# Tests for saturated tanh values moved ahead of the gate products, and those products written over the tanh values, in a fused attention and convolution-gated feed-forward kernel

## The chip, the cores and the metric

The kernel runs on one core of a Trainium2 chip. The metric is the device time of one execution in microseconds (us). The engines of the core are TensorE (PE in the profile, with its weight loads as PEld), VectorE (DVE), ScalarE (ACT), GpSimd (POOL) and SyncE (SP). They run side by side, each in the order of its own instruction list, and wait for one another through semaphores.

## The reference

Attention for 4 batches, 8 heads, 768 positions and a head width of 64, with a local window of 96 keys, 8 global keys and a bias that grows with distance; its heads side by side are the 512 columns of x. Then a feed-forward block with a gate that comes from a convolution along the sequence (w_in is 512 x 1024, w_out 1024 x 512, hp is h padded by one row at each end):

```python
    scores = np.where(keep, scores, -1000000000.0)
    scores = scores - np.max(scores, axis=-1, keepdims=True)
    a = np.exp(scores)
    a = a / (np.sum(a, axis=-1, keepdims=True) + 1e-09)
    return np.matmul(a, v).astype(np.float32)
...
    x = np.ascontiguousarray(attn_out.transpose(0, 2, 1, 3)).reshape(B, S, H * D)
...
    h = np.maximum(x @ w_in, 0.0)
    ...
    for k in range(K):
        conv_out += conv_w[k][None, None, :] * hp[:, k:k + S, :]
    gate = 1.0 / (1.0 + np.exp(-conv_out))
    return (h * gate @ w_out).astype(np.float32)
```

## The kernel before, in words

**Attention** runs as a pipeline of 96 steps: 32 jobs (a batch, a half of the sequence, a pair of heads) of three blocks of 128 queries. A step s goes through `scores` (L395, PE, into one of two PSUM buffers "s"), `maxima` (L412, DVE), `exps` (L426, ACT, into one of three buffers `pbuf`), `normalise` (L437 and L438 on DVE, L444 on POOL, in early steps also L442 on ACT), two steps later `transposes` (L452, PE, into one of two PSUM buffers "t"), `evict` (L457, ACT), and per job `values` (L473, PE), `mixed_high` (L485, ACT) and `mixed_low` (L489, DVE).

**The feed-forward block** runs in 8 units n = 0 to 7, one for each half sequence of 384 tokens. `mm1` (L507, PE) makes the features in 8 blocks f, each from three products of high and low parts of fp32 numbers; `relu` (L517, ACT) puts half of them into `hbuf`. `conv` (L557 on POOL or, in the first two units, L555 on ACT; then L558 and L559 on DVE) adds the three taps in the tile `c`, of which there is one buffer. `gate` (L577, ACT) takes the tanh of `c` in place, in four groups of two blocks. `saturated` (L588, ACT) reads the tanh values of one group once more and counts, in a column of `low`, how near they are to where an approximation would not hold; its elementwise result goes to a tile nobody reads (`sat`, tag "ob", which is also the only buffer of the output tiles of L629). `split` works on 128 tokens t at a time: L610 (DVE) makes (c + 1) * h, L612 (ACT) rounds it to `gh`, L613 (DVE) puts the rest into `gl`. `mm2` (L622, PE) multiplies both with the output weights in 24 products per 128 tokens; L629 evicts, L630 sends. The last 128 tokens of all go through `last_tile` (L643) and `leave` (L652, L655).

Where L610 writes is decided in `split`: over `h` in `hbuf` in the odd units and in parts that end before the unit does, over `c` in the last part of an even unit. As `saturated` reads `c`, a product that writes `c` has to wait for it.

**The order of work.** `ffn` writes a list of the unit's calls. A convolution, gate or test follows the products of a later block; what is left when `mm1` is over (`post`) is dealt out among the 24-product tiles of `mm2` of the unit before, at the positions that `AT` gives: the first row for even units, the second for odd ones.

```python
        at = AT[n % 2]
        for k, a in enumerate(mm):
            items.append(a)
            ...
            while post and at[-len(post)] <= k + 1:
                items.append(post.pop(0))
```

Unit 0 has no `mm2` beside it; its `post` is kept in `late` and runs within `mm1` of unit 1. The attention steps draw calls from this list. The first 16 steps stand in an order that is written out by hand; after them a scheduler orders each engine's list from the order of the calls, what they depend on and what it reckons that they take. Weight checks (L346 on DVE, L350 on ACT) and a final flag (L363 to L366, L895, L896) stand beside this; the flag is not waited for by the products.

Of the kernel before, what the change touches and what calls it, by code (L numbers as in the profile page):

```python
# [32 lines left out]
HF, NG = NF // 2, 4  # L33
NU, SPU = 2 * B, NPAIR * NB
# [11 lines left out]
DECODE_BY_HAND, DECODE_LATER = (0.3, 1.2), (1.35,)  # L46
FIRST_LOADS = (0, 0, 1, 2)
SHARE = (0.3, 0.5)
AT = ((2, 4, 9, 16, 17, 25), (1, 2, 4, 5, 7, 12, 16))


def key_columns(u):
# [15 lines left out]
def fast_path(tc, io):  # L68
# [422 lines left out]
    def ends(s):  # L491
        return s >= 0 and s % NB == NB - 1
# [72 lines left out]
    WG = NF // NG  # L565
# [27 lines left out]
    def split(n, t):  # L593
        b = n // 2
        t0, t1 = bounds[n % 2]
        a0, a1 = max(t0, t * P), min(t1, (t + 1) * P)
        if (b, t) not in gt:
            gt[b, t] = (
                pg.tile([P, NF, P], F32R, tag="gh", name=f"gh{b}_{t}"),
                pg.tile([P, NF, P], F32R, tag="gl", name=f"gl{b}_{t}"),  # L600
            )
        gh, gl = gt[b, t]
        c = cbuf[n][:, :, a0 - t0 : a1 - t0]
        sl = slice(a0 - t * P, a1 - t * P)
        h = hbuf[:, :, a0 + 1 : a1 + 1]
        if exact:
            V.scalar_tensor_tensor(c, c, 2.0, h, ALU.mult, ALU.mult)
        else:
            x = h if n % 2 or a1 < t1 else c
            V.scalar_tensor_tensor(x, c, 1.0, h, ALU.add, ALU.mult)  # L610
            c = x
        cur["gated"] = A.activation(gh[:, :, sl], c, AF.Copy)  # L612
        V.tensor_tensor(gl[:, :, sl], c, gh[:, :, sl].bitcast(F32), ALU.subtract)  # L613
# [44 lines left out]
    def ffn(n, defer=True):  # L658
        items = []
        add = lambda cost, fn, *a: items.append((cost, fn, a))  # L660
        early, lag = late[:], 1 + len(late) // 2
        late.clear()
        for f in range(NF):
            for part in range(3):
                if n or f >= EARLY or not begun[0]:
                    add(1, mm1, n, f, part)
                elif part == 0:
                    for k in range(begun[0], NK):
                        add(1, mm1_slice, f, k)
                if part == 1:  # L670
                    if early:
                        items.append(early.pop(0))
                    if f >= lag:
                        add(0, conv, n, f - lag)
                if part == 2:
                    g = f - lag + 1
                    if g > 0 and g % WG == 0:
                        add(0, gate, n, g // WG - 1)
                    g -= 1
                    if g > 0 and g % WG == 0 and n < NU - 1:  # L680
                        add(0, saturated, n, [g // WG - 1])
        old = tiles_of(n - 1) if n else []
        post = [(0, conv, (n, f)) for f in range(NF - lag, NF)] + [(0, gates, (n,))]
        post += [(0, split, (n, t)) for t in parts_of(n)]
        post.insert(len(post) if n == NU - 1 else lag + 3, (0, saturated, (n, range(NG))))
        mm = [(1, mm2, (b, t, f)) for b, t in old for f in range(NF)]
        if not mm and defer:
            late.extend(post[lag:])
            return items + post[:lag]
        if not mm:  # L690
            return items + post
# [3 lines that stand above are left out]
            if k == 0:  # L695
                for x in range(lag - 1):
# [3 lines that stand above are left out]
        return items + post  # L700

    def tiles_of(n):
        b = n // 2
        return [(b, t) for t in ((0, 1) if n % 2 == 0 else (2, 3, 4, 5))]

    def parts_of(n):
        return (0, 1, 2) if n % 2 == 0 else (2, 3, 4, 5)
# [77 lines left out]
    for s in range(len(steps) + LAG_V + 1):  # L785
        cur["s"] = s
        m, i = steps[s] if s < len(steps) else (len(jobs), -1)
        if s < HAND:
# [5 lines left out]
            x = (s - LAG_V - 1) // NB if ends(s - LAG_V - 1) else None  # L794
# [27 lines left out]
        else:  # L822
# [10 lines left out]
            if e >= 0:  # L833
                if e % SPU == SPU - 1:
                    queue.extend(ffn(e // SPU))
                left = SPU - (e + 1) % SPU + 1
                if e + 1 >= len(steps) - SPU:
                    left += 1
                k = -(-sum(cost for cost, _, _ in queue) // left)
# [67 lines left out]
    def general():  # L907
# [27 lines left out]
        for n in range(NU):  # L935
# [31 lines left out]
            for _, fn, a in ffn(n, defer=False):  # L967
                fn(*a)
# [98 lines left out]
```

## Time and profile before

| | |
|---|---|
| median of three runs | 446.5 us (445.61, 446.50, 447.54) |
| profiled execution, its own time | 445.31 us |
| its span on the core | 443.5 us, mean granted TensorE clock 0.996 |
| PE busy | 431.2 us, 97% of the span |
| DVE busy | 357.2 us, 81% |
| ACT busy | 309.9 us, 70% |
| POOL busy | 221.2 us, 50% |
| last PE instruction ends | 440.1 us into the span |

The span is what the profiler saw of one execution; 1.8 us of the execution's own time lie around it. Busy time is the time in which an instruction of an engine is under way. PE's matmuls overlap one another, so one that is listed with 0.40 us may start 0.23 us after the one before it.

### The profile page before, as it was taken

How to read it: one execution, taken by the hardware profiler on the slowest of the kernel's cores; microseconds unless marked ns; L12 is line 12 of the kernel's file. 1: busy time of each engine (PE TensorE's matmuls, PEld its weight loads, DVE VectorE, ACT ScalarE, POOL GpSimd, SP SyncE). 2: the span in 40 equal slices, each digit the busy share in tenths (PEclk: the TensorE clock that was granted, in tenths of full speed). 3: DMA queues.
4: the chain of work that ended last, by engine and by line, in shares of the span. 5: the costliest groups of instructions: out<-in, count | busy, mean ns of one | idle time of the engine just before them, and what ended most of it. 6: DMA issues, size and time to landing. Idle time of an engine off the chain costs nothing.

```text
span 443.5 us, 9050 instructions
## 1 busy us (share of the span) xinstructions
PE 431.2 (97%) x3039; PEld 374.5 (84%) x3039; DVE 357.2 (81%) x935; ACT 309.9 (70%) x839; POOL 221.2 (50%) x307
## 2 busy tenths in 40 slices
PE   8988999799999999999999999999999999999996
PEld 7655778799889988899889988899988998798876
DVE  6899899998999988757998989747999975568700
ACT  4889988789896678546876865665776776755540
POOL 5555334654456786556757744647656841013000
PEclk9999999899999999999999999999999999999999
DMA  6998953141543244442246134423235313980111
GB/s 210 294 255 258 271 184 110 40 163 65 153 128 120 75 136 132 128 125 94 85 128 192 41 107 145 141 102 104 67 119 181 103 48 122 312 295 32 47 49 55
DMA packets 22662, 60.02 MB, mean 135 GB/s; under 512 B 3024, under 2 KB 5584, under 8 KB 22608
## 3 DMA queue, kind: packets, MB, share of 16 engines
q1 hardware_dynamic: 18992, 53.01, 39.2%
q10 hardware_dynamic: 3616, 6.36, 3.9%
q8 instruction: 26, 0.43, 0.4%
q14 instruction: 28, 0.23, 0.2%
HBM read 53.07 MB, written 6.29 MB: 134 GB/s over the span
## 4 chain that ended last, share of the span: by engine, by line
PE 81%; DVE 8%; DMA 6%; ACT 3%; issue 1%; POOL 0%; SPq 0%; DVEq 0%; ACTq 0%
PE o L622 26%; PE h L507 25%; PE pv L473 10%; PE t L452 9%; PE s L395 7%; DMA check<-in_w 3%; PE s L385 1%; PE last L643 1%; DMA out<-ob 1%; DVE w L320 1%; DVE w L318 1%; ACT junkb L350 1%; ACT pbuf L426 1%; DMA rq<-in_qk 1%; PE sb L385 1%
## 5 line engine op out<-in xcount | busy, mean ns | idle before, releaser
L444 POOL TENSOR_SCALAR pbuf<-pbuf,mm 128x232 f32<-128x232 f32 (+1 forms) x160 | 113.3, 718 | 81.0 <-DVE mm L438 49.5
L426 ACT ACTIVATE pbuf<-s,mm 128x232 f32<-128x232 f32 (+1 forms) x165 | 72.1, 442 | 48.3 <-DVE mm L412 34.6
L412 DVE CUSTOM_DVE_ANT_0 s<-s,tab 128x232 f32<-128x232 f32 (+1 forms) x165 | 63.1, 385 | 20.2 <-PE s L395 15.7
L622 PE MATMUL o<-woh,gh 128*128 128x512 f32 x184 | 74.1, 403 | 0.0
L622 PE MATMUL o<-woh,gl 128*128 128x512 f32 x184 | 73.5, 400 | 0.0
L622 PE MATMUL o<-wol,gh 128*128 128x512 f32 x184 | 73.3, 398 | 0.0
L452 PE MATMUL t<-ident,pbuf 128*128 128x128 f32 x384 | 65.4, 279 | 5.4 <-ACT pbuf L442 2.7
L557 POOL TENSOR_SCALAR c<-hbuf,cw 128x382 f32<-128x382 f32 (+1 forms) x48 | 38.6, 807 | 56.5 <-ACT hbuf L517 56.5
L452 PEld LDWEIGHTS t<-ident,pbuf 128*128 128x128 f32 x384 | 46.4, 141 | 20.2 <-ACT pbuf L442 6.4
L457 ACT ACTIVATE pt<-t 128x512 f32<-128x512 f32 x96 | 57.0, 597 | 8.3 <-PE t L452 8.0
L507 PE MATMUL h<-xl,wih 128*128 128x384 f32 x252 | 59.4, 343 | 0.0
L507 PE MATMUL h<-xh,wih 128*128 128x384 f32 x252 | 58.8, 347 | 0.1
L507 PE MATMUL h<-xh,wil 128*128 128x384 f32 x252 | 55.8, 339 | 0.0
L473 PE MATMUL pv<-pt,v 128*64 128x128 f32 (+1 forms) x768 | 50.3, 280 | 0.3 <-DVE xl L489 0.2
L473 PEld LDWEIGHTS pv<-pt,v 128*64 128x64 f32 (+1 forms) x768 | 42.5, 138 | 8.6 <-issue 3.6
L558 DVE SCALAR_TENSOR_TENSOR c<-hbuf,cw,c 128x382 f32<-128x382 f32 (+1 forms) x64 | 44.3, 699 | 4.8 <-POOL c L557 3.7
L559 DVE SCALAR_TENSOR_TENSOR c<-hbuf,cw,c 128x382 f32<-128x382 f32 (+1 forms) x64 | 45.4, 712 | 0.3
L507 PEld LDWEIGHTS h<-xh,wih 128*128 128x128 f32 x252 | 43.2, 190 | 2.1 <-ACT pbuf L426 0.9
L507 PEld LDWEIGHTS h<-xl,wih 128*128 128x128 f32 x252 | 43.9, 189 | 0.7 <-issue 0.7
L507 PEld LDWEIGHTS h<-xh,wil 128*128 128x128 f32 x252 | 44.1, 188 | 0.0
L517 ACT ACTIVATE hbuf<-h 128x384 f32<-128x384 f32 x64 | 31.4, 495 | 13.5 <-PE h L507 12.5
L622 PEld LDWEIGHTS o<-woh,gl 128*128 128x128 f32 x184 | 34.6, 188 | 7.3
(120 smaller groups left out, 856.1 us busy)
## 6 DMA issues: line engine op xcount, KB each, us to landing
v<-in_vv SPq DMA_DIRECT2D x32, 384.0 KB, 3.6
rq<-in_qk SPq DMA_DIRECT2D x23, 384.0 KB, 3.1
wr<-in_w SPq DMA_DIRECT2D x16, 512.0 KB, 5.3
check<-in_w SPq DMA_DIRECT2D x16, 512.0 KB, 4.9
rk<-in_qk SPq DMA_DIRECT2D x12, 504.0 KB, 3.6
out<-ob ACTq DMA_DIRECT2D x23, 256.0 KB, 2.4
rk<-in_qk SPq DMA_DIRECT2D x11, 408.0 KB, 3.6
rq<-in_qk SPq DMA_DIRECT2D x16, 96.0 KB, 5.1
```

What stands on the lines that cost most here:

```text
L412: last_ttr[s] = V.tensor_tensor_reduce(out=sp[j][:, c0 : c0 + n], in0=sp[j][:, c0 : c0 + n], in1=tb, scale=-0.125, scalar=3.0e38, op0=ALU. ...
L426: last_exp[s] = A.activation(pb[:, j, c0 : c0 + n], sp[j][:, c0 : c0 + n], AF.Exp, bias=mm[:, j : j + 1], scale=-1.0, accum_out=mm[:, 2 + ...
L444: G.tensor_scalar(x, x, inv, 1.0, ALU.mult, ALU.mult)
L452: T.transpose(pt[:, j, c, :], pb[:, j, c * P : (c + 1) * P], ident)
L457: last_ev[s] = A.activation(sb, st_pt[s], AF.Copy)
L473: T.matmul(pv[m][64 * j : 64 * j + 64, i * P : (i + 1) * P], vt[m][:n, i, c, 64 * j : 64 * j + 64], sb[:n, j, c, :], start=c == 0, stop=c ...
L507: T.matmul(ps[:, :TB], w_[:, k, fs], x_, start=part == 0 and k == 0, stop=part == 2 and k == NK - 1,)
L517: A.activation(half, ps[:, :TB], AF.Relu, scale=0.5)
L557: G.tensor_scalar(c, *tap(1), 1.0, ALU.mult, ALU.mult)
L558: V.scalar_tensor_tensor(c, *tap(0), c, ALU.mult, ALU.add)
L559: V.scalar_tensor_tensor(c, *tap(2), c, ALU.mult, ALU.add)
L622: last = T.matmul(ps, g_[:, f], w_[:, f], start=f == 0 and part == 0, stop=f == NF - 1 and part == 2,)
```

## The change

Three edits, in code that decides the order and one operand:

- `saturated` is called for all four groups right after the gates, before any `split` of the unit; before, it stood after the first two splits, and in the last unit after all of them. In the last unit it is now also called within `mm1`, as in the others.
- `AT` has new numbers, since the call has another place in `post`.
- The product (c + 1) * h is written over `c` in units 0 to 6 and over `h` in unit 7. L612 and L613 read it from there.

```diff
-AT = ((2, 4, 9, 16, 17, 25), (1, 2, 4, 5, 7, 12, 16))
+AT = ((2, 4, 5, 9, 16, 25), (1, 2, 4, 6, 7, 12, 16))
...
-            x = h if n % 2 or a1 < t1 else c
+            x = h if n == NU - 1 else c
             V.scalar_tensor_tensor(x, c, 1.0, h, ALU.add, ALU.mult)
             c = x
...
-                    if g > 0 and g % WG == 0 and n < NU - 1:
+                    if g > 0 and g % WG == 0:
                         add(0, saturated, n, [g // WG - 1])
...
         post = [(0, conv, (n, f)) for f in range(NF - lag, NF)] + [(0, gates, (n,))]
+        post += [(0, saturated, (n, range(NG)))]
         post += [(0, split, (n, t)) for t in parts_of(n)]
-        post.insert(len(post) if n == NU - 1 else lag + 3, (0, saturated, (n, range(NG))))
```

The built lists of every engine are the same up to what runs at about 93 us; from there the scheduler puts instructions elsewhere. Three places follow.

**First place, PE, where unit 1 goes from `mm1` to the first `mm2` of unit 0** (about 112 us of the trace). o_0 is the first output tile, t_ are transposes of three attention steps in turn (1584, 1632, 1692), s_1714 the scores of a later one. Before, t_1584 stands earlier, within `mm1`, and the list goes on:

```order
L622 MATMUL o_0_1749<-woh,gl_0_1430 128x512
L395 MATMUL s_1714<-kk_1503,qh_1501 128x232
L395 MATMUL s_1714<-kk_1503,ql_1502 128x232
L395 MATMUL s_1714<-kk_1503,qh_1501 128x232
L395 MATMUL s_1714<-kk_1503,ql_1502 128x232
L622 MATMUL o_0_1749<-woh,gh_0_1429 128x512
L622 MATMUL o_0_1749<-wol,gh_0_1429 128x512
L452 MATMUL t_1632<-ident,pbuf_194 128x128 x4
L452 MATMUL t_1692<-ident,pbuf_195 128x128 x4
L622 MATMUL o_0_1749<-woh,gl_0_1430 128x512
```

Now:

```order
L622 MATMUL o_0_1749<-woh,gl_0_1461 128x512
L452 MATMUL t_1584<-ident,pbuf_193 128x128 x4
L452 MATMUL t_1632<-ident,pbuf_194 128x128 x4
L452 MATMUL t_1692<-ident,pbuf_195 128x128 x4
L395 MATMUL s_1714<-kk_1500,qh_1498 128x232
L395 MATMUL s_1714<-kk_1500,ql_1499 128x232
L395 MATMUL s_1714<-kk_1500,qh_1498 128x232
L395 MATMUL s_1714<-kk_1500,ql_1499 128x232
L622 MATMUL o_0_1749<-woh,gh_0_1460 128x512
```

The three transposes have come together, with no other product between them.

**The same place on ACT.** pt_1589 is the eviction of t_1584; pbuf_193 is the buffer that t_1584 reads and that the exps of s_1602 write next. Before:

```order
L426 ACTIVATE pbuf_193,mm_1607<-s_1602,mm_1607 128x136
L457 ACTIVATE pt_1589<-t_1584 128x512
L426 ACTIVATE pbuf_193,mm_1607<-s_1602,mm_1607 128x136
L555 ACTIVATE c_1541<-hbuf,cw 128x386
L517 ACTIVATE hbuf<-h_6_1653 128x384
L485 ACTIVATE xh_1677<-pv_1616 128x384
L577 ACTIVATE c_1541<-c_1541 128x772
L588 ACTIVATE sat_0_1651,misc<-c_1541,misc 128x772
```

Now:

```order
L485 ACTIVATE xh_1677<-pv_1616 128x384
L577 ACTIVATE c_1541<-c_1541 128x772
L588 ACTIVATE sat_0_1651,misc<-c_1541,misc 128x772
L426 ACTIVATE pbuf_193,mm_1607<-s_1602,mm_1607 128x136
L457 ACTIVATE pt_1589<-t_1584 128x512
L426 ACTIVATE pbuf_193,mm_1607<-s_1602,mm_1607 128x136
L555 ACTIVATE c_1541<-hbuf,cw 128x386
L517 ACTIVATE hbuf<-h_6_1653 128x384
```

The first gate and test of unit 1 have moved ahead of these exps and of the eviction between them.

**Second place, ACT at the last gates of unit 1** (about 127 us). The exps of the scores with the number 1822 (1823 in the changed kernel) free the PSUM buffer that the scores s_1903 want. Before:

```order
L588 ACTIVATE sat_2_1861,misc<-c_1541,misc 128x772
L426 ACTIVATE pbuf_194,mm_1827<-s_1822,mm_1827 128x232 x2
L577 ACTIVATE c_1541<-c_1541 128x772
L426 ACTIVATE pbuf_195,mm_1874<-s_1869,mm_1874 128x232 x2
L588 ACTIVATE sat_3_1863,misc<-c_1541,misc 128x772
```

Now:

```order
L588 ACTIVATE sat_2_1810,misc<-c_1541,misc 128x772
L577 ACTIVATE c_1541<-c_1541 128x772
L426 ACTIVATE pbuf_194,mm_1828<-s_1823,mm_1828 128x232 x2
L588 ACTIVATE sat_3_1812,misc<-c_1541,misc 128x772
L426 ACTIVATE pbuf_195,mm_1874<-s_1869,mm_1874 128x232
```

The last gate has changed places with those exps. On PE, the values of one job that stood right ahead of s_1903 have moved behind it.

**Third place, ACT in the last unit** (about 408 to 425 us). Before:

```order
L577 ACTIVATE c_5154<-c_5154 128x772
L612 ACTIVATE gh_2_5078<-hbuf 128x8x2
L612 ACTIVATE gh_3_5333<-hbuf 128x1024
L629 ACTIVATE ob_0_5352<-o_0_5302 128x512
L612 ACTIVATE gh_4_5344<-hbuf 128x1024
L630 DMA out<-ob_0_5352 128x512
L612 ACTIVATE gh_5_5368<-hbuf 128x1024
L629 ACTIVATE ob_1_5385<-o_1_5355 128x512
L630 DMA out<-ob_1_5385 128x512
L588 ACTIVATE sat_0_5388,misc<-c_5154,misc 128x772
L588 ACTIVATE sat_1_5390,misc<-c_5154,misc 128x772
```

Now:

```order
L588 ACTIVATE sat_1_5259,misc<-c_5154,misc 128x772
L517 ACTIVATE hbuf<-h_6_5261 128x384
L577 ACTIVATE c_5154<-c_5154 128x772
L517 ACTIVATE hbuf<-h_7_5285 128x384
L588 ACTIVATE sat_2_5306,misc<-c_5154,misc 128x772
L577 ACTIVATE c_5154<-c_5154 128x772
L588 ACTIVATE sat_3_5333,misc<-c_5154,misc 128x772
L612 ACTIVATE gh_2_5078<-hbuf 128x8x2
L612 ACTIVATE gh_3_5347<-hbuf 128x1024
L629 ACTIVATE ob_0_5355<-o_0_5308 128x512
```

All four tests now stand among the last gates, ahead of the roundings and of the output tiles.

## Rows read from the trace of the kernel before

**Rows 1.** The page: span, and busy time of each engine.

```profile
span 443.5 us, 9050 instructions
...
PE 431.2 (97%) x3039; PEld 374.5 (84%) x3039; DVE 357.2 (81%) x935; ACT 309.9 (70%) x839; POOL 221.2 (50%) x307
```

**Rows 2.** Windows: length, busy PE, PEld, DVE, ACT, POOL; PE clock, DMA share, GB/s.

```profile
0.00:44.35 44.35, 37.97 (x360) 27.78 (x361) 38.23 (x141) 34.20 (x115) 24.95 (x57) 1.00 0.86 254
...
94.00:440.20 346.20, 345.90 (x2341) 307.47 (x2339) 271.64 (x670) 232.69 (x596) 172.23 (x222) 1.00 0.38 119
440.20:443.50 3.30, 0.00 (x0) 0.00 (x0) 0.00 (x0) 0.37 (x1) 0.00 (x0) 1.00 0.15 47
```

**Rows 3.** Timeline of PE at its two longest idle times (start, us, what, idle before).

```profile
39.41 0.44 PE L452 MATMUL t<-ident,pbuf 128*128 128x128 f32 x2 [1.04 <-DMA rq<-in_qk]
...
84.15 0.38 PE L395 MATMUL s<-kk,qh 128*128 128x232 f32 x1 [2.06 <-ACT pbuf L426]
```

**Rows 4.** Window right behind the second of them, columns as in rows 2.

```profile
85.30:88.70 3.40, 3.40 (x29) 3.07 (x26) 3.40 (x8) 1.93 (x6) 0.55 (x1) 0.51 0.00 1
```

**Rows 5.** Groups of DVE, shapes apart: count, busy us, mean ns, idle before.

```profile
L610 DVE SCALAR_TENSOR_TENSOR hbuf<-c,hbuf 128x1024 f32<-128x1024 f32 x20 | 26.2, 1332 | 0.7 <-ACT c L577 0.7
...
L610 DVE SCALAR_TENSOR_TENSOR c<-c,hbuf 128x1008 f32<-128x1008 f32 x4 | 5.9, 1481 | 1.7 <-ACT sat L588 1.7
```

**Rows 6.** Waits: who for whom, us in total, times, longest.

```profile
ACT sat L588 <- DMA out<-ob: 3.2, 2, 2.1
...
DVE c L610 <- ACT sat L588: 1.7, 1, 1.7
```

**Rows 7.** Chain that ended last, 105 to 135 us (start, us, what).

```profile
112.18 0.70 PE o L622 x3
112.88 0.44 PE s L395 x4
...
113.79 0.87 PE t L452 x8
...
126.94 1.47 PE pv L473 x24
128.41 0.65 PE s L395 x4
```

**Rows 8.** Timeline of ACT, 107 to 132 us.

```profile
108.44 0.35 ACT L426 ACTIVATE pbuf<-s,mm 128x136 f32<-128x136 f32 x1
...
108.79 0.58 ACT L457 ACTIVATE pt<-t 128x512 f32<-128x512 f32 x1
...
111.11 0.85 ACT L577 ACTIVATE c<-c 128x772 f32<-128x772 f32 x1
111.99 0.94 ACT L588 ACTIVATE sat<-c,misc 128x772 bf16<-128x772 f32 x1
...
127.07 0.45 ACT L426 ACTIVATE pbuf<-s,mm 128x232 f32<-128x232 f32 x1
```

**Rows 9.** Timeline of POOL, 104 to 134 us.

```profile
119.93 0.89 POOL L444 TENSOR_SCALAR pbuf<-pbuf,mm 128x232 f32<-128x232 f32 x2 [0.17 <-DVE mm L438]
...
128.09 4.50 POOL L444 TENSOR_SCALAR pbuf<-pbuf,mm 128x232 f32<-128x232 f32 x4 [0.98 <-DVE mm L438]
```

**Rows 10.** Timeline of DVE, 129 to 133 us.

```profile
129.71 2.63 DVE L610 SCALAR_TENSOR_TENSOR hbuf<-c,hbuf 128x16 f32<-128x16 f32 x3
```

**Rows 11.** Last unit: timeline of ACT, 409 to 418 us.

```profile
411.21 0.85 ACT L577 ACTIVATE c<-c 128x772 f32<-128x772 f32 x1 [2.03 <-DVE c L559]
412.32 0.22 ACT L612 ACTIVATE gh<-hbuf 128x16 fp32r<-128x16 f32 x1 [0.25 <-DVE hbuf L610]
413.51 1.08 ACT L612 ACTIVATE gh<-hbuf 128x1024 fp32r<-128x1024 f32 x1 [0.97 <-DVE hbuf L610]
```

**Rows 12.** Last unit: timeline of DVE, 411 to 420 us.

```profile
415.61 2.44 DVE L613 TENSOR_TENSOR gl<-hbuf,gh 128x16 fp32r<-128x16 f32 x3
```

**Rows 13.** Chain that ended last, 400 to 444 us.

```profile
406.14 24.73 PE o L622 x106
```

## The prediction

> **What bounds the kernel now.** I read the page first: PE is busy for 97% of the span, DVE for 81%, ACT for 70% [rows 1]. Then the windows by stage. From 94 us to 440.2 us PE is busy for 345.90 of 346.20 us, while DVE has 74.56 us to spare there and ACT 113.51; before that, up to 44.35 us, PE idles for 6.38 us; behind 440.2 us there is a tail of 3.30 us with no product in it [rows 2]. As the built lists are the same up to about 93 us, the change acts on the full stretch alone. There the end comes where PE's list ends, and four things can move it: PE waits for something, PE's clock falls, the products follow one another at another spacing, or the tail grows. Time saved on ACT or DVE isn't one of them, unless PE waits less for it, and of that only 0.30 us is there to be had.
>
> **The change, part by part.**
>
> *Where the product is written.* 17 of the 20 wide L610 that wrote over h (all but the three of unit 7) now write over c, and L613 reads there. The old form took 1332 ns on average, the form that writes c 1481 [rows 5]. If all of that difference were due to the operand, 17 x 0.149 = 2.5 us of DVE work would come on top, in a stretch where DVE has 74.56 us to spare [rows 2]; if none, nothing. I take nothing: the idle time of DVE covers either, and without that cover the price is at most the 2.5 us, spread over 17 places.
>
> *The wait that goes with it.* A product over c must wait for all four tests of its unit. Before, four products did, and once this cost DVE 1.7 us [rows 6]. Behind a waiting L610 stand DVE's maxima and reciprocals of the attention steps, then the exps on ACT, then the transposes on PE. What keeps the wait short is the order of the calls: with the new positions the last test is called at least two feature blocks ahead of the first product of the unit (at 4 against 6 in odd units, 5 against 9 in even ones), and two blocks are 6 products of PE at 24.73 / 106 = 0.233 us [rows 13], thus 1.4 us against one test of 0.94 [rows 8]. I take nothing for PE; if the cover were gone, 1.7 us at a place.
>
> *The tests' own wait.* A test writes its junk into the one output tile, and twice ACT waited for that tile's transfer, 3.2 us in all [rows 6]. With the tests ahead of the output tiles this should be gone from ACT. It stood off PE's path (PE's idle time in the whole stretch is 0.30 us), so the gain is 0, at most that 0.30.
>
> *First place, about 112 us.* This is where I expect the change to be felt. In the new order of PE the three transposes t_1584, t_1632 and t_1692 follow each other. There are two PSUM buffers for them, so t_1692 waits for the eviction of t_1584. That eviction stands in ACT's list behind the first exp of s_1602, which in turn writes the buffer that t_1584 reads. So, from the end of t_1584: an exp (start to start 108.79 - 108.44 = 0.35 us) and an eviction of 0.58 [rows 8], 0.93 in all plus what passing from engine to engine costs; PE has only t_1632 to do meanwhile, half of the 0.87 us that eight of these products took [rows 7], thus 0.44. The difference is 0.49, without the hand-overs between the engines, which no row prices alone. ACT itself must be there in time: gate and test, 0.85 and 0.94 [rows 8], have moved ahead, and in my walk down its list they end about when t_1584 does; half a microsecond more would make it 1.0. Before, scores of 0.44 us and two products stood there [rows 7], and nothing was waited for. I take 0.75, the middle of 0.49 and 1.0; the lowest end is 0 (ACT's list runs far ahead of my walk, so that the exp is not held up by it and t_1692 comes later anyway).
>
> *Second place, about 127 us.* The scores s_1903 need the PSUM buffer that the exps of s_1823 free. Before, those exps ended at 127.07 + 0.45 = 127.52 [rows 8] and the scores came at 128.41, behind values of 1.47 us that began at 126.94 [rows 7]. Now the values come later, so PE asks for the scores at 126.94; and the gate, 0.85 [rows 8], stands ahead of the exps, which puts their end at 128.37, less whatever ACT gains by an eviction of 0.58 and a test's part that now stand elsewhere. The upper end is so 128.37 - 126.94 - 0.58 = 0.85; the lower is 0, if ACT comes a gate's length earlier to this place. I take the middle, 0.45.
>
> *The last unit.* All four tests now stand among the last gates. ACT idles there: 2.03 us ahead of the last gate, 0.97 ahead of the second wide rounding [rows 11]. A test and its read-out is 0.94 us [rows 8], so the third fits into the first of these, and the fourth goes between the last gate (done at 412.06) and the rounding at 412.32, which it delays by some 0.8 us; the wide one at 413.51 waits for L610 anyway. PE begins with this unit's own tile after 48 of the 106 products, at 406.14 + 48 x 0.233 = 417.3 [rows 13], and the first of the low parts that it needs comes out of the batch that starts at 415.61 [rows 12], at about 415.8. So 1.5 us is to spare and 0.8 is used. I cost it at 0; from 1.5 us of delay on, each further one would cost its length. The tail hangs on the last products and stays.
>
> The trace of before shows no change of spacing that I could book, see the rivals.
>
> **The sum.** 0.75 + 0.45 = 1.2 us, bounds 0 and 1.85. The profiled execution took 445.3 us (1.8 of it outside the span), so it would be 446.5. The three runs of before have their median 1.2 us above that execution; against this median the forecast is 446.5 + 1.2 = 447.7 us. What a measurement can tell from no change is about 0.5%, 2.2 us; the forecast is no change by that bound.
>
> **The rivals.**
>
> *The stall cools PE (slower).* At 84.15 us PE idles for 2.06 us [rows 3], and the 3.40 us from 85.30 on are run at a granted clock of 0.51, the 1.2 GHz level [rows 4]: about 0.49 x 3.40 = 1.7 us lost on top. If the first place did the same, the time would be 447.7 + 1.7 = 449.4. Against it: 1.04 us of idle time at 39.41 [rows 3] lies in a stretch whose clock is 1.00 [rows 2]. The point that decides lies between 1.04 and 2.06 us of idle time in one place, and my upper end for the first place is 1.0. The Trainium skill, "TensorE: Matmul & The Clock Gate", section "What's actually happening", says that the throttle is the default and that activity holds it open, which agrees with the fall at 84 us and would let a stall cost more than its own length. Chance 0.13.
>
> *DVE products meet the normalising on POOL (slower).* Two L444 took 0.89 us at 119.93, but four took 4.50 at 128.09, while three L610 ran from 129.71 [rows 9, 10]. That is 4.50 - 4 x 0.445 = 2.7 us by which a step's transposes may come late. The products are the same in number after the change, but lie beside other steps; where a step has less than 2.7 us to spare, PE waits. It happened before without PE waiting, as the chain there shows [rows 7], which speaks against. At one place with a margin of half of it, 447.7 + 1.35 = 449.0. The Trainium skill, "SBUF — State Buffer", section "Who interferes with whom", has the rule: a DVE instruction with two inputs in SBUF contends with a GpSimd instruction that reads SBUF, and the loser is blocked for the whole instruction. The rows fit it, and it holds for c as for h, so it makes no difference which of them is written. Chance 0.07.
>
> *Nothing reaches PE (no change).* ACT's list runs ahead of my walk at both places; the sum is 0, the time 446.5, or 446.2 with the 0.30 us of idle time gone. Chance 0.22.
>
> *A smoother list of PE (faster).* The new list changes less often between kinds of products (436 runs of one line before, 422 after). Scores that followed values took 0.65 us, others 0.44 [rows 7]; if each of the 14 switches that are gone had cost that 0.21, 2.9 us would be gained: 447.7 - 2.9 = 444.8. Against it: the dear kind is the one behind values, and these are as many as before; the other pieces of the chain (0.70 for three, 0.44 for four) are not longer for a switch. Chance 0.08.
>
> The forecast itself has the remaining 0.50, with a range of its own of 446.5 to 448.4 (its bounds). Faster by over 0.5%, below 444.3: the smoother list together with the gain of ACT's waits, 0.07. Slower by over 0.5%, above 448.7: the two slower rivals, of which 0.02 falls short, 0.18. Within: 0.75. The range takes in the cold stall and the case of nothing with the scatter of the runs of before, 0.9 us down: 445.3 to 449.8; it leaves the smoother list out.
>
> **What would show it.** In the changed kernel PE should idle for 0.5 to 1.0 us shortly before 114 us, ahead of a transpose, with the eviction on ACT as what ended it, and for up to 0.9 us near 127 us ahead of scores, ended by exps. The waits of the tests for the output's transfer should be gone, those of L610 for the tests should be there without any of PE behind them, and PE should run from the last unit's first output product to the end without a gap. The prediction is wrong if PE idles for more than 2 us in all after 94 us, if the clock drops in any window there, or if the stretch from 94 to the last product is shorter than before by more than 0.5 us: then the spacing of products, not waits, was what could be won.

## The result: 0.9% slower, and the profile after

| | before | after |
|---|---|---|
| median | 445.89 us (8 runs, 444.99 to 447.54) | 450.51 us (8 runs, 448.13 to 451.91) |
| ratio of the runs | | 1.0093, 95% interval 1.0066 to 1.0120 |
| profiled execution, its span | 445.31, 443.5 us | 450.98, 449.2 us |
| mean granted clock in it | 0.996 | 0.991 |

The forecast was 447.7 us with a range up to 449.8, and no change. By the ratio the kernel got slower by 4.1 us (2.9 to 5.4), by the medians by 4.6; the measured median lies outside of the range, and the loss is clear of no change.

The page of the changed kernel, against [rows 1]:

```profile
span 449.2 us, 9050 instructions
...
PE 432.5 (96%) x3039; PEld 375.7 (84%) x3039; DVE 354.0 (79%) x935; ACT 307.4 (68%) x839; POOL 222.8 (50%) x307
```

The work is the same; PE is busy 1.3 us longer in a span that is 5.7 us longer. To see where, take two products that both lists have: the first output product of unit 0's tiles (112.02 us before) and the last one of unit 1's (188.92). The windows around and between them, first of the kernel before, then of the changed one (columns as in [rows 2]):

```profile
94.00:112.02 18.02, 18.02 (x132) 17.46 (x131) 16.62 (x37) 16.89 (x45) 6.55 (x8) 1.00 0.34 105
112.02:188.92 76.90, 76.90 (x537) 67.00 (x536) 69.41 (x175) 56.91 (x149) 49.10 (x60) 1.00 0.41 124
188.92:443.50 254.58, 250.99 (x1678) 223.01 (x1676) 185.61 (x459) 159.27 (x403) 116.58 (x155) 1.00 0.37 117
```

```profile
94.00:113.68 19.68, 19.68 (x156) 18.94 (x155) 18.96 (x40) 16.82 (x44) 8.82 (x9) 1.00 0.33 103
113.68:194.07 80.39, 77.56 (x536) 67.18 (x536) 69.10 (x176) 58.31 (x157) 47.90 (x59) 1.00 0.36 116
194.07:449.20 255.13, 251.12 (x1680) 223.52 (x1678) 182.38 (x461) 157.44 (x403) 119.14 (x155) 1.00 0.36 117
```

The stretch from 112 to 189 us took 76.90 us and takes 80.39: 3.49 us more for the same 536 or 537 products, with 2.83 us in which PE idles, where there were none. The rest, six units, takes 0.55 us more. The remaining 1.66 us lie ahead of the first output product. They are not the change's: a run below with the whole change in units 0 to 6 reached that product at 111.95 us, and then needed 80.41 us for the same stretch. In the profiled execution of the changed kernel the clock fell early, 0.69 between 26 and 30 us, where the other ran at 1.00.

PE's idle times behind 94 us, in its timeline (start, us, what, idle before and what ended it), one line for each that is over 0.25 us:

```profile
115.94 0.63 PE L452 MATMUL t<-ident,pbuf 128*128 128x128 f32 x4 [0.54 <-ACT pt L457]
...
130.42 0.38 PE L395 MATMUL s<-kk,qh 128*128 128x232 f32 x1 [0.72 <-ACT pbuf L426]
...
142.04 0.44 PE L507 MATMUL h<-xl,wih 128*128 128x384 f32 x1 [1.57 <-DVE xl L489]
...
407.44 0.97 PE L507 MATMUL h<-xh,wih 128*128 128x384 f32 x4 [0.65 <-ACT hbuf L517]
```

The first two are the ones that were forecast, at their places and with the releasers that were named. The third was not, and is the largest. The next lines show what stands ahead of its releaser in DVE's list, in the timeline of DVE:

```profile
131.91 2.90 DVE L610 SCALAR_TENSOR_TENSOR c<-c,hbuf 128x16 f32<-128x16 f32 x3
...
135.04 1.24 DVE L610 SCALAR_TENSOR_TENSOR c<-c,hbuf 128x1024 f32<-128x1024 f32 x1
...
136.45 1.30 DVE L613 TENSOR_TENSOR gl<-c,gh 128x16 fp32r<-128x16 f32 x2
137.78 1.21 DVE L141 TENSOR_TENSOR kk<-rk,kk 64x1008 fp32r<-64x1008 f32 x1
139.02 1.73 DVE L613 TENSOR_TENSOR gl<-c,gh 128x1024 fp32r<-128x1024 f32 x1
...
141.44 0.54 DVE L489 TENSOR_TENSOR xl<-pv,xh 128x384 fp32r<-128x384 f32 x1
```

This L489 makes the low part of the last attention result that unit 2 takes in, and each block of unit 2's first products has one product that needs it; PE had begun three blocks when it came to the first of these. Its high part L485 was through at 137.93 us (ACT, 137.42 and 0.51 long), but DVE had four products and three low parts of unit 1 ahead of it. In the kernel before, the same L489 ran at 132.83 us, between the third and the fourth product and ahead of all low parts:

```profile
129.71 2.63 DVE L610 SCALAR_TENSOR_TENSOR hbuf<-c,hbuf 128x16 f32<-128x16 f32 x3
...
132.83 0.55 DVE L489 TENSOR_TENSOR xl<-pv,xh 128x384 fp32r<-128x384 f32 x1
133.30 0.16 DVE L613 TENSOR_TENSOR gl<-hbuf,gh 128x16 fp32r<-128x16 f32 x1
...
135.23 1.37 DVE L610 SCALAR_TENSOR_TENSOR hbuf<-c,hbuf 128x1024 f32<-128x1024 f32 x1
```

The values that this L489 takes its low part from came on PE at 126.87 us before and at 134.14 now, thus 14.85 and 20.46 us behind the first output product:

```profile
126.87 1.54 PE L473 MATMUL pv<-pt,v 128*64 128x128 f32 x24
```

```profile
134.14 1.54 PE L473 MATMUL pv<-pt,v 128*64 128x128 f32 x24
```

So two things moved against each other: the values later on PE, the products and low parts of unit 1 closer together on DVE.

### The profile page after: what moved, and what is told of

It reads as the page before. It is cut to its first block, busy times and chain, and to the rows that moved or that the text cites. A ratio compares the mean times of both kernels' runs of the same rounds, so it can differ in the third digit from the quotient of the medians.

```text
span 449.2 us, 9050 instructions
## 1 busy us (share of the span) xinstructions
PE 432.5 (96%) x3039; PEld 375.7 (84%) x3039; DVE 354.0 (79%) x935; ACT 307.4 (68%) x839; POOL 222.8 (50%) x307
## 4 chain that ended last, share of the span: by engine, by line
PE 74%; DVE 15%; DMA 4%; ACT 4%; issue 2%; POOL 0%; SPq 0%; ACTq 0%; DVEq 0%
PE o L622 25%; PE h L507 23%; PE pv L473 9%; PE t L452 8%; PE s L395 6%; DMA check<-in_w 3%; DVE c L558 2%; DVE s L412 2%; ACT pbuf L426 1%; PE s L385 1%; PE last L643 1%; DVE c L559 1%; DVE gl L613 1%; DVE kk L141 1%; DVE w L318 1%
## 5 line engine op out<-in xcount | busy, mean ns | idle before, releaser
L444 POOL TENSOR_SCALAR pbuf<-pbuf,mm 128x232 f32<-128x232 f32 (+1 forms) x160 | 116.1, 735 | 91.8 <-DVE mm L438 60.7
L452 PE MATMUL t<-ident,pbuf 128*128 128x128 f32 x384 | 64.4, 278 | 6.0 <-ACT pbuf L442 3.1
L457 ACT ACTIVATE pt<-t 128x512 f32<-128x512 f32 x96 | 57.9, 603 | 8.8 <-PE t L452 8.2
L507 PE MATMUL h<-xl,wih 128*128 128x384 f32 x252 | 58.5, 341 | 1.6 <-DVE xl L489 1.6
L557 POOL TENSOR_SCALAR c<-hbuf,cw 128x382 f32<-128x382 f32 (+1 forms) x48 | 36.2, 757 | 47.2 <-ACT hbuf L517 46.1
L507 PE MATMUL h<-xh,wil 128*128 128x384 f32 x252 | 57.0, 340 | 0.0
L558 DVE SCALAR_TENSOR_TENSOR c<-hbuf,cw,c 128x382 f32<-128x382 f32 (+1 forms) x64 | 44.1, 698 | 6.1 <-POOL c L557 5.3
L559 DVE SCALAR_TENSOR_TENSOR c<-hbuf,cw,c 128x382 f32<-128x382 f32 (+1 forms) x64 | 42.0, 660 | 0.4
```

The lines of the kernel that those rows point to most:

```text
L444: G.tensor_scalar(x, x, inv, 1.0, ALU.mult, ALU.mult)
L452: T.transpose(pt[:, j, c, :], pb[:, j, c * P : (c + 1) * P], ident)
L457: last_ev[s] = A.activation(sb, st_pt[s], AF.Copy)
L507: T.matmul(ps[:, :TB], w_[:, k, fs], x_, start=part == 0 and k == 0, stop=part == 2 and k == NK - 1,)
L557: G.tensor_scalar(c, *tap(1), 1.0, ALU.mult, ALU.mult)
L558: V.scalar_tensor_tensor(c, *tap(0), c, ALU.mult, ALU.add)
```

## The experiments

Most of the kernels below differ in two sets of units alone, written as one edit to the kernel before: NEW, the units that have the new order and the new positions, and OVER_C, those whose products write over `c`. With NEW = 0 to 7 and OVER_C = 0 to 6 the built lists are those of the changed kernel, with both empty those of before.

```diff
-AT = ((2, 4, 9, 16, 17, 25), (1, 2, 4, 5, 7, 12, 16))
+AT, AT_NEW, NEW, OVER_C = ...
...
-            x = h if n % 2 or a1 < t1 else c
+            x = c if n in OVER_C or not (n % 2 or a1 < t1) else h
...
-                    if g > 0 and g % WG == 0 and n < NU - 1:
+                    if g > 0 and g % WG == 0 and (n < NU - 1 or n in NEW):
...
-        post.insert(len(post) if n == NU - 1 else lag + 3, (0, saturated, (n, range(NG))))
+        post.insert(lag + 1 if n in NEW else len(post) if n == NU - 1 else lag + 3, (0, saturated, (n, range(NG))))
...
-        at = AT[n % 2]
+        at = (AT_NEW if n in NEW else AT)[n % 2]
```

The ratio and its interval are formed from the single runs, so it is not quite the quotient of the two medians. The last column is the stretch of the section above in the profiled execution of each, from the start of the first output product to the start of the last one of unit 1: 76.90 us before, 80.39 in the changed kernel. It leaves out the early part, where the clock differs from execution to execution, and the last unit.

| run | median, us | before beside it | ratio, 95% interval | stretch, us |
|---|---|---|---|---|
| units 0 and 1 changed | 450.34 | 445.00 | 1.0109, 1.0076 to 1.0141 | 80.41 |
| units 2 to 7 changed | 445.85 | 445.00 | 1.0014, 0.9997 to 1.0031 | 76.87 |
| order alone, all units | 448.19 | 445.00 | 1.0061, 1.0027 to 1.0096 | 78.88 |
| units 0 to 6 changed | 449.01 | 445.00 | 1.0093, 1.0067 to 1.0118 | 80.41 |
| unit 0 changed | 451.52 | 445.63 | 1.0113, 1.0079 to 1.0146 | 81.63 |
| units 1 to 7 changed | 446.95 | 445.63 | 1.0015, 0.9987 to 1.0042 | 77.29 |
| all, two low parts of unit 1 held | 448.01 | 445.63 | 1.0053, 1.0031 to 1.0075 | 79.30 |
| units 1 to 6 changed | 446.88 | 445.63 | 1.0022, 0.9999 to 1.0045 | 77.26 |
| all, first gate of unit 1 held | 449.19 | 445.42 | 1.0069, 1.0043 to 1.0095 | 80.00 |
| unit 7 changed | 446.24 | 445.42 | 1.0013, 0.9991 to 1.0034 | 76.93 |
| unit 0, order alone | 446.07 | 445.78 | 1.0011, 0.9986 to 1.0036 | 77.79 |
| all, unit 0's products as before | 447.88 | 445.43 | 1.0048, 1.0025 to 1.0072 | 78.35 |

### Which units: 0 and 1 against 2 to 7

```diff
+NEW, OVER_C = (0, 1), (0, 1)
```

> The whole change in units 0 and 1 alone; units 2 to 7 as before. Theory P (the loss sits in the passage from unit 1 to unit 2, where the re-sorted lists make PE stop three times: 0.54 us at 115.94, 0.72 at 130.42, 1.57 at 142.04, 2.8 us in all): about 2.8 to 3.5 us over the kernel before, with the same three stops. Rival O (every unit pays, because the products over the tanh tile wait for the tests): about a quarter of the 4.6 us, thus some 1.2 us. Rival L (the last unit's tests delay PE, 0.65 us at 407.44 in the changed kernel): nothing of it here.

Ratio 1.0109, and the three stops of PE are there to within a hundredth:

```profile
115.90 0.63 PE L452 MATMUL t<-ident,pbuf 128*128 128x128 f32 x4 [0.54 <-ACT pt L457]
...
130.38 0.38 PE L395 MATMUL s<-kk,qh 128*128 128x232 f32 x1 [0.71 <-ACT pbuf L426]
...
142.00 0.45 PE L507 MATMUL h<-xl,wih 128*128 128x384 f32 x1 [1.57 <-DVE xl L489]
```

```diff
+NEW, OVER_C = (2, 3, 4, 5, 6, 7), (2, 3, 4, 5, 6)
```

> The whole change in units 2 to 7, units 0 and 1 as before; the lists of PE are those of before through the passage to unit 2. Theory P: no stop of PE over 0.3 us between 94 and 390 us, time within 1 us of before (0.65 us from the last unit may remain). Rival O: three quarters of the loss, some 3.5 us over before. Rival L: 0.65 us and more over before.

Ratio 1.0014: none of the three stops, one of 1.36 us at 403.29, among unit 7's products. From 150 to 390 us, thus in units 2 to 6, the change costs PE nothing: it is busy for all of the 240 us.

```profile
150.00:390.00 240.00, 240.00 (x1683) 212.70 (x1682) 190.81 (x493) 162.46 (x432) 140.67 (x178) 1.00 0.37 118
```

So it is the passage (P), and not the wait of every product (O).

### The last unit

```diff
+NEW, OVER_C = (0, 1, 2, 3, 4, 5, 6), (0, 1, 2, 3, 4, 5, 6)
```

> The whole change but for unit 7, whose tests stand behind all of its products again. Theory P: 0.5 to 0.8 us better than the changed kernel, 3.5 to 4 us over before, with the three stops of the passage. Rival L: back to within 1 us of before. Rival O: like theory P, so this run does not tell these two apart.

Ratio 1.0093 again, with the three stops (0.54, 0.72 and 1.56 us) and one of 0.59 us at unit 7, though unit 7 is that of before. The 0.5 to 0.8 us that theory P expected to get back did not come. And unit 7 alone:

```diff
+NEW, OVER_C = (7,), ()
```

> The whole change in unit 7 alone; PE's list is that of before up to unit 7. Theory L2 (the early tests of unit 7 delay its relus on ACT and make PE stop for 0.6 to 1.6 us near 402): 0.6 to 1.5 us over before, with that stop. Rival M (the stop there comes and goes with when the weights for the checks arrive, whether or not the tests are early, as the run with unit 0 alone, whose unit 7 is that of before, had 0.51 there): within 0.5 us of before, a stop of 0 to 0.6.

Ratio 1.0013, and no stop of PE over 0.2 us behind 94 us. Its chain from 395.88 us on is PE alone:

```profile
395.88 9.88 PE h L507 x57
405.76 22.39 PE o L622 x96
...
428.27 5.79 PE o L622 x24
434.06 5.67 PE last L643 x48
```

Theory L2 falls: the early tests of the last unit cost PE nothing by themselves. The stop at 400 to 410 us was between none and 1.63 us in the runs, and it was there (0.59) with unit 7 as before and absent with unit 7 changed. The relu that ended it stood behind other work on ACT, and what ACT itself had waited for there was not the same everywhere: in the changed kernel it idled for 1.14 us for a convolution (L559) ahead of a gate, a weight check and a test; in the run with units 0 to 6 changed for 1.78 us, and with unit 0 alone for 0.82 us, for the transfer of a weight check. So the checks' arrival (rival M) fits some of these stops and not others. No run separates the two, and what makes the stop come and go stays open.

### The two parts of the change

```diff
+NEW, OVER_C = (0, 1, 2, 3, 4, 5, 6, 7), ()
```

> Tests early and the new positions in all units, but the products are written where they were before. Theory P in the form that the early tests and gates alone re-sort the lists: stops of 1 to 3 us in all in the passage, 1 to 3.5 us over before; here the transposes t_1584 stand early again and the values of one job stand ahead of s_1903 as before, so the first two stops should be gone, and the third (the low part L489 of that job still stands behind three products and two low parts of unit 1 in the list of DVE) should be left or be larger. Rival O: within 0.5 us of before, since no product waits for tests but those that did.

Ratio 1.0061. The first two stops are gone, as expected from the list. The expected third stop is not there either, though L489 stands behind products and low parts of unit 1 in this list too; the values come ahead of s_1903 as before. Instead PE stopped for 0.98 and 0.30 us near 125 us on POOL's normalising, which the expectation did not have, and for 0.70 and 0.40 us at unit 7. The order alone makes another list with other stops.

### Which of units 0 and 1

The built lists of before and after part at one instruction: the last test of unit 0, which on ACT now stands eight places earlier, ahead of L485 and the first relus of unit 1.

```diff
+NEW, OVER_C = (0,), (0,)
```

> The whole change in unit 0 alone; units 1 to 7 as before. The built lists show that the re-sorting of the passage from unit 1 to unit 2 begins with one instruction: the last test of unit 0 on ACT stands eight places earlier, ahead of a rounding of attention results and of the first relus of unit 1. Theory U (unit 0's early test re-sorts what follows, and that is the loss): the first two stops of PE as in the changed kernel (0.5 us of idle time near 114, 0.7 near 129), the third in some form (1 to 2 us: the low part L489 stands behind even more products of unit 1 in DVE's list), 3 to 4.5 us over before. Rival V (unit 1's own early tests make the stops): within 1 us of before.

Ratio 1.0113: the change in unit 0 alone loses as much as the whole change. The first two stops are those of the changed kernel; where the third was, there are several smaller ones, of which two end on POOL's normalising:

```profile
115.57 0.63 PE L452 MATMUL t<-ident,pbuf 128*128 128x128 f32 x4 [0.54 <-ACT pt L457]
...
130.05 0.38 PE L395 MATMUL s<-kk,qh 128*128 128x232 f32 x1 [0.70 <-ACT pbuf L426]
...
137.82 0.44 PE L452 MATMUL t<-ident,pbuf 128*128 128x128 f32 x2 [0.92 <-POOL pbuf L444]
...
139.20 0.44 PE L452 MATMUL t<-ident,pbuf 128*128 128x128 f32 x2 [0.50 <-POOL pbuf L444]
...
142.94 1.54 PE L473 MATMUL pv<-pt,v 128*64 128x128 f32 x24 [0.69 <-issue]
```

```diff
+NEW, OVER_C = (1, 2, 3, 4, 5, 6, 7), (1, 2, 3, 4, 5, 6)
```

> The whole change in units 1 to 7; unit 0 as before. Theory U: PE's list is that of before up to unit 2 but for small things, so no stop over 0.3 us between 94 and 390 us; 0 to 1.4 us over before (unit 7's relus may make PE stop for 0.6 to 1.4). Rival V: 3 to 4 us over before with the stops near 114, 129 and 141.

Ratio 1.0015: with unit 0 as before, the other seven units can have the change, and what is left of the loss is 0.7 us, with an interval from -0.6 to 1.9. One stop of 0.53 us on L489 at 134.91 us is left of the third, which theory U did not expect, and 1.07 us at unit 7.

```diff
+NEW, OVER_C = (0,), ()
```

> The smallest part: in unit 0 alone the tests are called ahead of its products (in ACT's list this moves one test by eight places at first, and the scheduler re-sorts from there); the products write where they did before, units 1 to 7 are as before. Theory U1 (that one early test is enough): the list of PE is that of the run with the order alone up to the second output tile, so the stop at 125 us that ended on the normalising of POOL (0.98 us and 0.30) comes back, and the time is 1.5 to 3.5 us over before. Rival X (it needs the product over the tanh tile as well): within 0.7 us of before, no stop over 0.3 us between 94 and 390 us.

Ratio 1.0011: the early test alone, with the products of unit 0 where they were, costs nothing that the times can tell; in its profile the stretch is 0.89 us longer than before, with 0.29 us of idle time at 128 us. Theory U1 falls and rival X holds: PE's list has the stop's place, but the stop did not come back at its size.

```diff
+NEW, OVER_C = (0, 1, 2, 3, 4, 5, 6, 7), (1, 2, 3, 4, 5, 6)
```

> The changed kernel, but in unit 0 the products write where they did before; its tests stay early, and units 1 to 7 have the whole change. Theory U2 (both parts together in unit 0 make the list with the three stops; the early test alone does not): no stop of 0.5 and 0.7 us near 114 and 129 that ends on the eviction and on the exps, none of 1.6 near 141; 2 to 4 us below the changed kernel, 0 to 2 us over before (the list of PE is that of the run with the order alone up to the second output tile, which had 1.3 us of stops at 125). Rival Y (the early test in unit 0 together with the rest of the change elsewhere is enough): as the changed kernel, 4 to 5 us over before.

Ratio 1.0048, about half of the loss, and none of the three stops; 0.30 and 0.34 us on POOL's normalising near 126 and 140, 0.83 us at unit 7. Theory U2 holds and rival Y falls. So the early tests do not make the three stops without the products over `c` in unit 0. The reverse, products over `c` with the tests where they were, has not been run. It is also open through which dependency the products act: written over `c`, they wait for the test, but they also make L612 and L613 read `c`, of which there is one buffer, so that the next unit's convolution has to wait for those too. The timeline of ACT in unit 1's first blocks shows what the scheduler made of it. Before, the roundings of unit 0 stood between the first relus and the last test behind them:

```profile
96.10 1.07 ACT L612 ACTIVATE gh<-hbuf 128x1024 fp32r<-128x1024 f32 x1
97.07 0.49 ACT L517 ACTIVATE hbuf<-h 128x384 f32<-128x384 f32 x1
97.44 1.07 ACT L612 ACTIVATE gh<-hbuf 128x1024 fp32r<-128x1024 f32 x1
...
99.96 0.95 ACT L588 ACTIVATE sat<-c,misc 128x764 bf16<-128x764 f32 x1
```

In the changed kernel the test comes first, and the roundings follow three of the relus:

```profile
95.84 0.93 ACT L588 ACTIVATE sat<-c,misc 128x764 bf16<-128x764 f32 x1
...
97.13 0.49 ACT L517 ACTIVATE hbuf<-h 128x384 f32<-128x384 f32 x1
...
97.88 0.50 ACT L517 ACTIVATE hbuf<-h 128x384 f32<-128x384 f32 x1
98.69 0.49 ACT L517 ACTIVATE hbuf<-h 128x384 f32<-128x384 f32 x1 [0.31 <-PE h L507]
99.08 1.05 ACT L612 ACTIVATE gh<-c 128x1024 fp32r<-128x1024 f32 x1
```

```diff
+NEW, OVER_C = (1, 2, 3, 4, 5, 6), (1, 2, 3, 4, 5, 6)
```

> The whole change in units 1 to 6; units 0 and 7 as before. Theory U with the last unit's stop as the rest: no stop over 0.3 us between 94 us and the end but the one at the last unit's start that the run with all units but the last showed (0.6 us), so within 0.7 us of before, and 0 to 0.8 us better than with unit 7 changed. If early tests gained anything in the middle units it would show here as a time below before.

Ratio 1.0022: nothing gained in the middle units, as in the run of units 2 to 7. Against the expectation the stop on L489 is there with 0.53 us, at 136.12 us; 0.64 us stand at unit 7.

### The third stop by itself

In the changed kernel, two low parts of unit 1 are called behind the L489 that PE waits for. Nothing is left out.

```diff
-        V.tensor_tensor(gl[:, :, sl], c, gh[:, :, sl].bitcast(F32), ALU.subtract)
+        low_part = lambda: V.tensor_tensor(gl[:, :, sl], c, gh[:, :, sl].bitcast(F32), ALU.subtract)
+        held.append(low_part) if n == 1 and t in (3, 4) and not exact else low_part()
...
-                mixed_low(e // NB)
+                x_low = mixed_low(e // NB)
+                if e // NB == 11:
+                    with tc.issue_after(x_low.ins):
+                        while held:
+                            held.pop(0)()
```

> The changed kernel, but two low parts of unit 1 (L613 of its second and third 128 tokens) are called behind the low part L489 that PE waits for at the third stop; nothing is left out. Theory D (the third stop is DVE's list: L489 stands behind 3 products and 3 low parts of unit 1): L489 comes 2.4 to 2.9 us earlier, the third stop (1.57 us idle, 1.9 with what restarting costs) is gone, the first two stay; 1.5 to 2.2 us below the changed kernel. Rival W (the late values, which came 7 us later in PE's list, and their rounding on ACT set it): L489 would start at once when its rounding is done, about 138 us, whether or not the list is freed; as it started at 141.44 in the changed kernel, three and a half microseconds behind that rounding, this is thought unlikely, and then the stop stays.

Ratio 1.0053 against 1.0093 for the changed kernel: 1.8 us back (0.0040 x 446), though the two intervals overlap. The stretch tells it more sharply: 79.30 us against 80.39, 1.09 us back. Its timeline of DVE:

```profile
135.28 1.20 DVE L141 TENSOR_TENSOR kk<-rk,kk 64x1008 fp32r<-64x1008 f32 x1
...
137.48 0.54 DVE L489 TENSOR_TENSOR xl<-pv,xh 128x384 fp32r<-128x384 f32 x1
137.94 2.79 DVE L613 TENSOR_TENSOR gl<-c,gh 128x1024 fp32r<-128x1024 f32 x2
```

L489 starts 4.12 us after the first instruction behind the batch of three products (133.36), in the changed kernel 6.71 us after it (134.73): 2.6 us earlier by the list. The third stop is gone, the first two are there (0.81 and 0.68 us). The two low parts that were held made no other stop in the stretch. Theory D holds: with the values as late as they are here, the third stop is made by the order of DVE's list. That the stretch got back 1.09 us and not the whole stop is in part the first stop, which grew by 0.27 us: here the exp ahead of the eviction of t_1584 stood right behind gate and test and began 0.77 us after t_1584 did (112.73 and 113.50 us), in the changed kernel 0.47 us after it (114.37 and 114.84). At unit 7 PE stopped for 1.63 us in this profile.

### The first two stops by themselves

```diff
-            A.activation(c, c, AF.Tanh)
+            with tc.issue_after(last_ev[30].ins) if (n, k) in ((1, 0),) and 30 in last_ev else contextlib.nullcontext(): A.activation(c, c, AF.Tanh)
```

> The changed kernel, but the first gate of unit 1 is called behind the eviction of t_1584; nothing is left out. In ACT's list the exp of s_1602 and that eviction now stand ahead of gate and test, and at the second place the exps that free the buffer of s_1903 stand ahead of the last gate again; PE's three transposes still follow each other. Theory A (gate and test, 1.8 us on ACT, hold up the eviction at the first stop): the first stop is gone. Theory B (the first stop is the chain transpose, exp, eviction, transpose, since in the changed kernel ACT was free at 114.78 us, just as t_1584 ended): it stays at about 0.5 us. Both: the second stop, 0.72 us, is gone or under 0.2. The third place has another list again and isn't forecast; 0.5 to 2 us below the changed kernel.

Ratio 1.0069. ACT was idle for 2.84 us, and PE stopped all the same, first in ACT's, then in PE's timeline:

```profile
114.11 0.37 ACT L426 ACTIVATE pbuf<-s,mm 128x136 f32<-128x136 f32 x1 [2.84 <-PE t L452]
...
114.47 0.59 ACT L457 ACTIVATE pt<-t 128x512 f32<-128x512 f32 x1
```

```profile
113.64 1.03 PE L452 MATMUL t<-ident,pbuf 128*128 128x128 f32 x8
115.20 0.63 PE L452 MATMUL t<-ident,pbuf 128*128 128x128 f32 x4 [0.53 <-ACT pt L457]
116.20 0.38 PE L395 MATMUL s<-kk,qh 128*128 128x232 f32 x1 [0.37 <-ACT pbuf L426]
```

Theory B holds, A falls: the first stop is the chain of transpose, exp, eviction and transpose behind a list that puts three transposes in a row. The second stop, at s_1903, is gone; a new one, 0.37 us, came at the scores behind the transposes, one of 1.09 at the values of 141 us, and one of 1.23 at unit 7.

No version was faster than the kernel before.

## Why the prediction was wrong

**What bounds the kernel** was right: the loss is time in which PE idles between 112 and 189 us (2.83 of 3.49 us), while DVE has no more to do there than before (69.10 us, before 69.41).

**The first place** was right in place and mechanism, and in size partly by luck. It was booked at 0.75 us: PE idles for 0.54, and from the start of the eight transposes (114.37) to the next (115.94) there are 1.57 us instead of 0.87 [rows 7], 0.70 lost. That the chain alone makes this stop was then shown by holding the gate. The booked middle went halfway to an ACT that comes late, which had no part in the changed kernel's profile; what filled about the same room were the hand-overs between the engines, which the prediction named and left unpriced: 1.57 us from start to start against 0.44 + 0.35 + 0.58 = 1.37 for the pieces that it had rows for. ACT's lateness is not without weight, though: with the two low parts held it came 0.3 us late, and the stop was 0.81.

**The second place** was right in mechanism; the term was too small. It was booked at 0.45 between 0 and 0.85; 0.72 us of idle time stand in the trace, 0.87 from start to start.

**The wait that goes with it** is the step that failed, at "I take nothing for PE". It priced how long a product would wait for a test and named maxima and reciprocals as what stands behind it. It did not follow L489, which stands in the same list, nor ask what PE would need of DVE first once the values had moved "later", as the second place has it. The values' low part is that. DVE's waits of L610 for tests were 3.2 us in five places, but they are not what PE paid: with the two low parts held, the products still wait, 2.7 us in four places, and the stop is gone. The missing term is 1.57 us of idle time; taking it out made the stretch 1.09 us shorter. The prediction's own sign of being wrong, more than 2 us of idle time after 94 us, came in with 3.48.

**The forecast as a sum.** Measured from start to start, as at the first place, the three stops cost 0.70, 0.87 (129.33 to 130.42 for two transposes of 0.22) and 1.73 us (139.79 to 142.04 for three products of 0.52), 3.3 in all, against the 1.2 that were booked. The stretch lost 3.49 and the units behind it 0.55, 4.04 in all, where the ratio says 4.1. The 4.6 of the medians lies within the scatter of the runs (448.13 to 451.91), which goes in part with the clock: the execution with a mean of 0.999 took 448.13 us, the one with 0.989 took 451.91.

**The tests' own wait** for the transfer of the output tile is gone from the waits, and nothing was gained: right. **Where the product is written**: wide L610 over `c` took 1298 ns on average, over `h` 1217 in unit 7 (1332 before, [rows 5]); booked at nothing, and by these rows the operand itself costs nothing. But in unit 0 it does decide the list, and that was not considered. **The last unit**: PE ran without a gap from its first output product on, as forecast; a stop of 0.65 us ahead of that came from a relu of unit 7, which stood behind a gate, a check and a test; the run with unit 7 alone has no such stop.

**The rivals.** The stall did not cool PE: the clock was 1.00 from 94 us to the last unit through idle times of 0.54, 0.72 and 1.57 us. But the bracket on which that rival was built, a deciding point between 1.04 and 2.06 us of idle time, does not hold in the later profiles (last section). POOL's normalising ended none of the three stops, but it ended the stops that other lists had in the same passage (0.92 and 0.50 us with unit 0 alone, 0.98 with the order alone). Ahead of that last one two L444 took 2.13 us from 123.97 us on, while L141, a DVE instruction of two inputs, ran from 123.83; two had taken 0.89 at 119.93 [rows 9]. So the rival's picture came up in other lists, and beside another instruction than L610; no run separates it from the rest. The smoother list did not show: with fewer switches, the time from 189 us on is the same but for the stop at 407 us.

## What to carry to other kernels

Where a scheduler orders the lists, a change of one test's place and one operand in one unit can cost more than all the work it touches: compare the built lists over the whole passage behind the first difference, and follow every instruction that PE will wait for, not only those that the diff names. A result that PE needs next should not stand behind a batch that nobody needs soon; calling two low parts behind it took away a stop of 1.57 us. A part of a change that costs can be found by doing it unit by unit: here unit 0 alone cost 1.1%, the other seven together 0.15%, which is within the noise. And where the early part of an execution scatters, the time between two products that all lists have tells kernels apart more sharply than the whole time: three runs with the same lists of units 0 and 1 gave 80.39, 80.41 and 80.41 us.

## What was not expected of the hardware

In all fourteen profiles PE's clock was 1.00 from 94 to 440 us, through stops of up to 1.63 us. Ahead of 94 us it fell for a few us in thirteen of them, and the length of the stop just before does not decide it. The kernel before and the one with units 1 to 6 changed have the same order of work there, and PE idled for 1.04 us up to 39.41 and 39.42 us, and for 2.06 us up to 84.15 and 85.72 us. Before, the clock held after the short stop and fell to the 1.2 GHz level after the long one; in the other kernel it was the other way round (windows around both stops, somewhat longer than the time at the lower level; columns as in [rows 2], first of the kernel before):

```profile
39.40:43.00 3.60, 3.59 (x35) 2.50 (x36) 3.57 (x15) 3.12 (x11) 2.52 (x3) 1.00 0.83 222
84.00:88.00 4.00, 3.62 (x30) 3.09 (x31) 4.00 (x10) 2.70 (x9) 1.36 (x2) 0.67 0.02 7
```

```profile
39.40:43.00 3.60, 3.58 (x28) 2.85 (x30) 3.57 (x15) 2.68 (x9) 2.52 (x3) 0.59 0.89 226
84.00:88.00 4.00, 2.05 (x28) 1.82 (x28) 4.00 (x11) 3.44 (x11) 2.92 (x3) 1.00 0.37 104
```

So in these runs a stop of 2.06 us was once without loss of clock and one of 1.04 us once was not; what decides between the executions is not shown. The clock of the first stage differs between executions of one order in the same way: in 26 to 30 us it was 0.69 in the changed kernel's profile, 0.73 with unit 0 changed, 0.50 with unit 0's order alone, and 1.00 in the eleven others. The first output product came at 111.28 us where the clock held throughout (units 1 to 7 changed), at 113.68 in the changed kernel and at 115.52 with unit 0's order alone.
